# One tile for each PSUM bank of the fill work, and new durations for the scheduler, in an attention kernel with a gated long convolution

The kernel computes an attention layer and a gated convolution behind it. While attention runs, everything else ("fill work") passes through two PSUM banks. The change gives each of these banks a tile of its own, where before two banks were the halves of one tile, and it puts new durations into the small scheduler that orders the instructions.

## Chip, cores, metric

One core of a Trainium2 chip. The metric is the device time of one execution in microseconds (us), lower is better. An execution over 1.5% longer than the kernel's fastest counts as slow. PSUM is the memory that PE writes its products to, used here as eight banks of 512 f32 columns; to evict a bank is to copy it out to SBUF, where the operands lie. Engines: PE multiplies matrices (PEld is its weight load), ACT and DVE work on elements and evict PSUM, POOL works, in this kernel, on elements in SBUF only, SP issues loads and stores.

## The reference

```python
# B,H,S,D = 4,8,768,64; 16 centroids per head
q_assign, k_assign = argmax of normalised q, k against the head's centroids
mask   = q_assign[:, :, :, None] == k_assign[:, :, None, :]
scores = where(mask, q @ k.T / sqrt(D), -1e9)
attn   = softmax(scores) @ v
x      = attn, heads side by side                        # (4, 768, 512)
x1, x2, x3 = split(x @ w_proj)                           # three of 512
conv   = irfft(rfft(x2) * rfft(filter))                  # along the sequence
out    = (x1 * conv * x3) @ w_out
```

The kernel works on 8 groups of 4 heads, two head pairs in each. A pair has 6 steps of 128 keys; a step takes two score products (one per head), an exp on each, and one output product over both. So there are 96 steps. The convolution is done as products with sine and cosine tables.

## The kernel before

The kernel is recorded as a list of operations with planned durations. A list scheduler (`place`) plays them through and fixes the order of the instructions on each engine and the PSUM banks. Semaphores are put in later, by the recording layer, from what each instruction reads and writes.

```python
T.ps = [pp.tile([128, 2, 512], F32, name=f"ps{i}") for i in range(4)]   # 8 banks as 4 pairs

def banks_for(bank, free, st, o):
    if bank.cls == "score":          # both halves of pair 0 or 1
        two = min(((0, 1), (2, 3)), key=lambda p: max(free[p[0]], free[p[1]]))
        return two if max(free[two[0]], free[two[1]]) < 1e8 else None
    if bank.cls == "o":              # output of a head pair
        return (4, 5) if max(free[4], free[5]) < 1e8 else None
    allowed = [6, 7]                 # fill work
    if st.score == 0 and bank.cls == "head":
        allowed += [0, 1, 2, 3, 4, 5]
    elif st.score == st.scores:
        allowed += [0, 1, 2, 3]
        if st.odone == st.otiles:
            allowed += [4, 5]
    ids = sorted((i for i in allowed if free[i] < 1e8), key=lambda i: (free[i], i))[:bank.n]
    return tuple(ids) if len(ids) == bank.n else None

def ap(h):                           # the bank of a fill operation: half of a pair
    return T.ps[h.ids[0] // 2][:, h.ids[0] % 2]
```

A typical fill operation is the projection of the convolution's input, 24 matmuls per batch in six groups of four. Each group fills a bank, and ACT or DVE evicts it:

```python
op(("PE", .87), U, due, r=[...], w=[h], alloc=h)            # 4 matmuls into ap(h)
op(EV512, lambda e, ...: copy(e, T.uv2[:, e_, m], ap(h)), due + 1, r=[h], w=[...], free=[h])
# ... the scheduler frees bank h.ids 0.06 us after the eviction ends, and knows nothing of pairs
```

The softmax here doesn't subtract the row's maximum and nothing guards it: scores larger than these inputs give would overflow.

## Time and profile before

| | |
|---|---|
| time, median of 3 | 521.73 us (520.88 to 522.03) |
| PE busy | 427.9 of 519.7 us, 82% |
| first score, end of the last output product | 36.18 us, 456.99 us |

The page's busy times and its chain of waits (the work that ended last, followed back):

```profile
PE 427.9 (82%) x2444; PEld 179.7 (35%) x2444; DVE 355.5 (68%) x556; ACT 274.5 (53%) x420; POOL 90.5 (17%) x93
...
PE 59%; DVE 21%; ACT 9%; issue 5%; DMA 2%; POOL 1%; POOLq 0%; DVEq 0%; ACTq 0%; SPq 0%
```

Busy time by stretch: the head to the first score, the body to the last output product, the tail. After the stretch come its length and the busy us (with instruction count) of PE, PEld, DVE, ACT and POOL, then the granted PE clock, the DMA share and GB/s:

```profile
core 0: us, PE busy (x) PEld busy (x) DVE busy (x) ACT busy (x) POOL busy (x), PEclk, DMA share, GB/s
0.00:36.18 36.18, 21.61 (x123) 12.93 (x124) 24.59 (x57) 20.36 (x39) 12.59 (x45) 0.91 0.91 193
36.18:456.99 420.81, 361.69 (x2096) 146.98 (x2093) 304.24 (x457) 237.65 (x352) 61.59 (x38) 0.99 0.25 64
456.99:519.67 62.68, 44.62 (x227) 19.78 (x227) 26.66 (x44) 16.51 (x30) 16.27 (x11) 0.89 0.13 51
```

Read the second row: PE idles 420.81 - 361.69 = 59.1 us of the body. The timeline (start, duration, engine, line, operation; in brackets the idle time before it and what ended that) shows what such a hole is made of, in the projection:

```profile
145.50 1.90 PE L587 MATMUL ps<-wpj,uT 128*128 128x512 bf16 x8
...
147.44 0.58 ACT L203 CAST uv<-ps 128x512 bf16<-128x512 f32 x1 [2.04 <-PE ps L587]
...
148.07 1.02 PE L587 MATMUL ps<-wpj,uT 128*128 128x512 bf16 x4 [0.67 <-ACT uv L203]
...
149.13 0.58 ACT L203 CAST uv<-ps 128x512 bf16<-128x512 f32 x1 [1.11 <-PE ps L587]
149.77 1.02 PE L587 MATMUL ps<-wpj,uT 128*128 128x512 bf16 x4 [0.67 <-ACT uv L203]
...
150.83 0.58 ACT L203 CAST uv<-ps 128x512 bf16<-128x512 f32 x1 [1.11 <-PE ps L587]
151.47 1.02 PE L587 MATMUL ps<-wpj,uT 128*128 128x512 bf16 x4 [0.67 <-ACT uv L203]
```

PE waits 0.67 us for ACT, ACT waits 1.11 us for PE, in turn, with nothing else under way on either, though the scheduler gave the groups two banks. And the first eviction starts at 147.44, after all eight matmuls of two groups, not after its own four.

### The profile page before, as it was taken

How to read it: one execution, taken by the hardware profiler on the slowest of the kernel's cores; microseconds unless marked ns; L12 is line 12 of the kernel's file. 1: busy time of each engine (PE TensorE's matmuls, PEld its weight loads, DVE VectorE, ACT ScalarE, POOL GpSimd, SP SyncE). 2: the span in 40 equal slices, each digit the busy share in tenths (PEclk: the TensorE clock that was granted, in tenths of full speed). 3: DMA queues.
4: the chain of work that ended last, by engine and by line, in shares of the span. 5: the costliest groups of instructions: out<-in, count | busy, mean ns of one | idle time of the engine just before them, and what ended most of it. 6: DMA issues, size and time to landing. Idle time of an engine off the chain costs nothing.

```text
span 519.7 us, 6779 instructions
## 1 busy us (share of the span) xinstructions
PE 427.9 (82%) x2444; PEld 179.7 (35%) x2444; DVE 355.5 (68%) x556; ACT 274.5 (53%) x420; POOL 90.5 (17%) x93
## 2 busy tenths in 40 slices
PE   3777899999979787797978888888978799969944
PEld 2342333333323343333323343333423333324421
DVE  7667786798768585675657886676727877663640
ACT  4654468777645465465744466355844455514112
POOL 4220000000005220111003422020101512110541
PEclk9966999999999999999999999999999999979997
DMA  9989005416312132023610213013310000002003
GB/s 209 215 162 232 2 16 142 106 33 138 93 32 67 40 81 45 31 77 112 165 31 12 66 35 88 3 44 106 111 33 4 13 1 32 11 23 121 2 0 122
DMA packets 67226, 37.06 MB, mean 71 GB/s; under 512 B 56636, under 2 KB 62328, under 8 KB 67192
## 3 DMA queue, kind: packets, MB, share of 16 engines
q1 hardware_dynamic: 65992, 34.50, 25.5%
q0 software_dynamic: 1056, 2.10, 2.3%
q8 instruction: 19, 0.31, 0.3%
q14 instruction: 15, 0.12, 0.1%
q10 hardware_dynamic: 144, 0.03, 0.0%
HBM read 30.66 MB, written 6.48 MB: 71 GB/s over the span
## 4 chain that ended last, share of the span: by engine, by line
PE 59%; DVE 21%; ACT 9%; issue 5%; DMA 2%; POOL 1%; POOLq 0%; DVEq 0%; ACTq 0%; SPq 0%
PE ps L475 19%; PE ps L616 8%; PE ps L460 7%; PE ps L661 5%; PE ps L587 4%; PE ps L369 4%; DVE acc L485 4%; DVE tm L600 3%; PE ps L639 3%; PE ps L498 2%; PE ps L387 2%; ACT uv L203 2%; DVE x L623 2%; ACT qkT L203 1%; DMA qkraw<-in_q_dram 1%
## 5 line engine op out<-in xcount | busy, mean ns | idle before, releaser
L464 ACT ACTIVATE p<-ps 128x768 f32<-128x768 f32 x192 | 149.5, 812 | 63.5 <-PE ps L460 46.6
L475 PE MATMUL ps<-p,vraw 128*64 128x385 f32 x768 | 147.0, 503 | 0.4 <-ACT osb L490 0.2
L485 DVE TENSOR_TENSOR acc<-acc,p 128x768 f32<-128x768 f32 x128 | 125.9, 1024 | 6.9 <-ACT p L464 6.7
L460 PE MATMUL ps<-aug,aug 128*128 128x384 bf16 (+1 forms) x384 | 85.7, 331 | 6.6 <-ACT p L464 5.1
L475 PEld LDWEIGHTS ps<-p,vraw 128*64 128x64 f32 x768 | 47.3, 137 | 66.1 <-issue 63.1
L616 PE MATMUL ps<-xT,wpj 128*128 128x384 bf16 x256 | 48.5, 326 | 14.2 <-DVE x L205 3.4
L604 POOL TENSOR_TENSOR y<-tm 128x512 bf16<-128x512 f32 x24 | 36.3, 1520 | 120.2 <-DVE tm L600 119.6
L369 PE MATMUL ps<-ident,qkraw 128*128 128x128 f32 x192 | 36.0, 312 | 22.7 <-DMA qkraw<-in_q_dram 9.0
L649 POOL TENSOR_TENSOR y<-yy,x 128x768 bf16<-128x768 f32 x16 | 32.6, 2035 | 120.2 <-DVE yy L645 79.7
L460 PEld LDWEIGHTS <-aug 128*128 128x128 bf16 (+1 forms) x384 | 33.4, 98 | 50.8 <-issue 37.5
L205 POOL CAST aug<-qkT 64x768 bf16<-64x768 f32 x10 | 10.9, 1086 | 176.7 <-ACT qkT L203 160.4
L369 PEld LDWEIGHTS ps<-ident,qkraw 128*128 128x128 f32 x192 | 23.9, 156 | 43.3 <-ACT qkT L203 10.1
L616 PEld LDWEIGHTS <-wpj 128*128 128x128 bf16 x256 | 23.9, 97 | 41.3 <-issue 25.3
L485 DVE TENSOR_TENSOR acc<-p,p 128x768 f32<-128x768 f32 x32 | 30.1, 964 | 11.0 <-ACT p L464 5.5
L623 DVE TENSOR_TENSOR x<-ps,x 128x384 f32<-128x384 f32 x32 | 17.5, 554 | 25.1 <-PE ps L616 7.8
L600 DVE TENSOR_TENSOR tm<-ps,hm 128x512 f32<-128x512 f32 x48 | 30.9, 682 | 5.4 <-PE ps L347 2.3
L661 PE MATMUL ps<-wout,y 128*128 128x512 bf16 x96 | 25.9, 413 | 9.1 <-POOL y L649 5.2
L587 PE MATMUL ps<-wpj,uT 128*128 128x512 bf16 x96 | 23.3, 379 | 7.8 <-ACT uv L203 7.0
L203 ACT COPY qkT<-ps 128x384 f32<-128x384 f32 x44 | 20.5, 482 | 16.4 <-PE ps L369 12.5
L203 ACT COPY x<-ps 128x384 f32<-128x384 f32 x24 | 11.5, 479 | 33.0 <-PE ps L616 20.0
L203 ACT COPY ob<-ps 128x512 f32<-128x512 f32 x23 | 12.8, 591 | 22.1 <-PE ps L661 15.5
L203 ACT CAST uv<-ps 128x512 bf16<-128x512 f32 x21 | 12.2, 585 | 23.2 <-PE ps L587 18.8
(114 smaller groups left out, 404.5 us busy)
## 6 DMA issues: line engine op xcount, KB each, us to landing
qkraw<-in_q_dram SPq DMA_DIRECT2D x32, 192.0 KB, 5.1
qkraw<-in_k_dram SPq DMA_DIRECT2D x32, 192.0 KB, 4.4
vraw<-in_v_dram SPq DMA_DIRECT2D x8, 768.0 KB, 5.6
rb<-dr SPq DMA_DIRECT2D x30, 192.0 KB, 3.4
out_dram<-ob SPq DMA_DIRECT2D x11, 512.0 KB, 2.6
y<-in_moe_filter_fft_dram SPq DMA_DIRECT2D x4, 384.0 KB, 7.8
wpj<-in_moe_w_proj_dram POOLq DMA_DIRECT2D x1, 1536.0 KB, 11.7
aug<-ohT SPq DMA_DIRECT2D x64, 24.0 KB, 1.9
```

Of the source, the lines that this page charges most:

```text
L203: T.nc.scalar.copy(out, in_)
L369: T.nc.tensor.transpose(ap(h)[:, ts(t, 128)], T.qkraw[s][:, 3 * ch + t].rearrange("p h d -> p (h d)"), T.ident)
L460: T.nc.tensor.matmul(two(h)[:, ch, :384], ag[1][:K, ts(sk, 128)], ag[0][:K, ts(ch, 384)], start=True, stop=True)
L464: ex = op(("ACT", .82 + (1.28 if first[0] is None else 0)), lambda e, h=h, s=s: T.nc.scalar.activation(T.p[s][:, :S].rearrange("p (a b) -> ...
L475: T.nc.tensor.matmul(o[64 * hp:64 * hp + 64, ch, :385], T.vraw[aset][:, 2 * pr + hp, sk * D:(sk + 1) * D], T.p[slots[hp, sk]][:, 384 * ch: ...
L485: T.nc.vector.tensor_tensor(T.acc[hp], x, T.p[slots[hp, sk]][:, :S], op=Alu.add)
L587: T.nc.tensor.matmul(ap(h), f[:, e_, kt, ts(m, 128)], T.wpj[:, kt, DM:2 * DM], start=(kt == 0), stop=(kt == ND - 1))
L600: op(("DVE", .68), lambda e, i=i, cs=cs, r=r, h=h: T.nc.vector.tensor_tensor(T.tm[r][:, cs], ap(h), T.hm[:, i, 2 * r + cs], op=Alu.mult), ...
L604: op(("POOL", 1.36), lambda e, i=i, r=r: T.nc.gpsimd.tensor_tensor(T.y[:, i, r], T.tm[r][:, 0], T.tm[r][:, 1], op=Alu.add), due + 2, r=[(" ...
L616: T.nc.tensor.matmul(ap(h)[:, :384], T.wpj[:, kt, off + dt * 128:off + dt * 128 + 128], T.xT[xs][:, kt, ts(ch, 384)], start=(kt == 0), sto ...
L649: op(("POOL", 1.8), lambda e, dt=dt, xb=xb: T.nc.gpsimd.tensor_tensor(T.y2[:, dt], T.yy[:].rearrange("p t c -> p (t c)"), T.x3[xb][:].rear ...
L661: T.nc.tensor.matmul(ap(h), T.y2[:, kt, ts(2 * tt + e_, 128)], T.wout[:, kt], start=(kt == 0), stop=(kt == ND - 1))
```

## The change

The intent: guard each bank by itself, so that an eviction of one fill bank runs while PE fills the other; and let the scheduler plan with durations nearer to a trace's. The core of the diff (cuts marked):

```diff
-    T.ps = [pp.tile([128, 2, 512], F32, name=f"ps{i}") for i in range(4)]
+    T.bank, T.pair = {}, {}
+    for i in (6, 7):
+        T.bank[i] = pp.tile([128, 512], F32, name=f"bank{i}")
     def ap(h):
-        return T.ps[h.ids[0] // 2][:, h.ids[0] % 2]
+        return bank(h.ids[0])                       # T.bank[i][:]
+class Psum:   # banks 0-3 and 4-5: single tiles, then pairs while scores and outputs
+    ...       # need them, then single tiles again; each turn closes a pool and opens one
 def banks_for(bank, free, st, o):
-    if st.score == 0 and bank.cls == "head":
-        allowed += [0, 1, 2, 3, 4, 5]
+    if st.score == 0:
+        allowed += [0, 1, 2, 3] if bank.cls == "head" else []
+    ...
+    if st.o == 0:
+        allowed += [4, 5] if bank.cls == "head" else []
+    ...       # a first score, a first output and the first fill after them wait for the whole side
-    def place(self, free0, banks_for, switch=0.1, ...
+    def place(self, free0, banks_for, switch=0.08, ...
-            op(("DVE", 2.1), fn, due, ...           # angles of the tables
+            op(("DVE", 2.8), fn, due, ...
-            op(("PE", .84), sim, ...                # likeness to the centroids
+            op(("PE", 1.0), sim, ...
-            op(("PE", 1.28), pv, ...                # output product
+            op(("PE", 1.37), pv, ...
# ... six smaller ones: den .85->.9, rec .45->.52, bc .7->1.15, y 1.36->1.45, I 1.1->1.15, y2 1.8->1.9
```

More of the change, by code (lines that the diff above doesn't have):

```diff
@@ L81, in op, with place @@
         return o
-    def place(self, free0, banks_for, switch=0.1, wait=0.1, rate=215e3):
+    def place(self, free0, banks_for, switch=0.08, wait=0.1, rate=215e3):
         free = dict(free0)
@@ L87, in place @@
         pend = 0
-        st = SimpleNamespace(pool=0.0, dve=0.0, bw=0.0, last=None, score=0, scores=sum(
-            1 for o in self.ops if o.alloc is not None and o.alloc.cls == "score"), otiles=sum(
-            1 for o in self.ops if o.alloc is not None and o.alloc.cls == "o"), odone=0)
+        st = SimpleNamespace(pool=0.0, dve=0.0, bw=0.0, last=None, score=0, o=0, tail=0)
+        st.scores, st.otiles = (sum(o.alloc is not None and o.alloc.cls == c for o in self.ops) for c in ("score", "o"))
         busy = dict.fromkeys(free, 0.0)
@@ L113, in place @@
                             continue
-                        t = max(t, max(bank_free[i] for i in ids))
+                        t = max(t, ids[1])
                     if o.lock and e == "DVE":
@@ L130, in place @@
             if o.alloc is not None:
-                o.alloc.ids = banks_for(o.alloc, bank_free, st, o)
+                o.alloc.ids = banks_for(o.alloc, bank_free, st, o)[0]
                 for i in o.alloc.ids:
@@ L134, in place @@
                 st.score += o.alloc.cls == "score"
+                st.o += o.alloc.cls == "o"
+                if o.alloc.cls not in ("score", "o"):
+                    st.tail |= (st.score == st.scores and min(o.alloc.ids) < 4) + 2 * (
+                        st.o == st.otiles and any(i in (4, 5) for i in o.alloc.ids))
             d = o.eng[e]
@@ L158, in place @@
                         bank_free[i] = h.end + 0.06
-                    if h.cls == "o":
-                        st.odone += 1
             for x in o.eng:
@@ L173, in banks_for, with whole @@
 def banks_for(bank, free, st, o):
+    def whole(lo, hi):
+        return max(free[lo:hi])
     if bank.cls == "score":
         two = min(((0, 1), (2, 3)), key=lambda p: max(free[p[0]], free[p[1]]))
-        return two if max(free[two[0]], free[two[1]]) < 1e8 else None
+        t = max(free[two[0]], free[two[1]]) if st.score else whole(0, 4)
+        return (two, t) if t < 1e8 else None
     if bank.cls == "o":
-        return (4, 5) if max(free[4], free[5]) < 1e8 else None
-    allowed = [6, 7]
-    if st.score == 0 and bank.cls == "head":
-        allowed += [0, 1, 2, 3, 4, 5]
-    elif st.score == st.scores:
-        allowed += [0, 1, 2, 3]
-        if st.odone == st.otiles:
-            allowed += [4, 5]
-    ids = sorted((i for i in allowed if free[i] < 1e8), key=lambda i: (free[i], i))[:bank.n]
-    return tuple(ids) if len(ids) == bank.n else None
+        t = whole(4, 6)
+        return ((4, 5), t) if t < 1e8 else None
+    allowed, first = [6, 7], []
+    if st.score == 0:
+        allowed += [0, 1, 2, 3] if bank.cls == "head" else []
+    elif st.score == st.scores:
+        if st.tail & 1:
+            allowed += [0, 1, 2, 3]
+        elif whole(0, 4) < 1e8:
+            first += [0, 1, 2, 3]
+    if st.o == 0:
+        allowed += [4, 5] if bank.cls == "head" else []
+    elif st.o == st.otiles:
+        if st.tail & 2:
+            allowed += [4, 5]
+        elif whole(4, 6) < 1e8:
+            first += [4, 5]
+    t = lambda i: whole(*((0, 4) if i < 4 else (4, 6))) if i in first else free[i]
+    ids = sorted((i for i in allowed + first if free[i] < 1e8), key=lambda i: (t(i), i))[:bank.n]
+    return (tuple(ids), max(map(t, ids))) if len(ids) == bank.n else None
 def build(T):
@@ L207, in ap, with bank @@
     def ap(h):
-        return T.ps[h.ids[0] // 2][:, h.ids[0] % 2]
+        return bank(h.ids[0])
+    def bank(i):
+        return T.bank[i][:]
     def two(h):
-        return T.ps[h.ids[0] // 2]
+        return T.pair[h.ids[0] // 2]
     EV384 = {"ACT": .48, "DVE": .55}
@@ L280, in fn @@
                 V.scalar_tensor_tensor(r, n, -1.0, n, op0=Alu.mult, op1=Alu.min)
-            op(("DVE", 2.1), fn, due, r=["kc", "s0t", ("x3", 0, 0), ("x3", 0, 1)], w=w, lock=True)
+            op(("DVE", 2.8), fn, due, r=["kc", "s0t", ("x3", 0, 0), ("x3", 0, 1)], w=w, lock=True)
             def sin(e, m=m):
@@ L388, in sim @@
                                        T.qkT[z][:, ch], start=True, stop=True)
-            op(("PE", .84), sim, due, r=[("qkT", z, ch) for z in range(4)] + ["cbd"], w=[h], alloc=h)
+            op(("PE", 1.0), sim, due, r=[("qkT", z, ch) for z in range(4)] + ["cbd"], w=[h], alloc=h, kind="sim")
             op(EV384, lambda e, ch=ch, h=h: copy(e, T.sim[:, ch], ap(h)[:, :384]), due + .8, r=[h], w=[("sim", ch)],
@@ L478, in pv @@
                                            start=(sk == 0), stop=(sk == NT - 1))
-            op(("PE", 1.28), pv, due, r=[("p", slots[0, sk]), ("p", slots[1, sk]), ("vraw", aset), "eps"] +
+            op(("PE", 1.37), pv, due, r=[("p", slots[0, sk]), ("p", slots[1, sk]), ("vraw", aset), "eps"] +
                ([ob] if sk else []), w=[ob], alloc=None if sk else ob, kind="pv")
@@ L499, in den @@
                                        start=True, stop=True)
-        op(("PE", .85), den, te + .5, r=[("acc", 0), ("acc", 1), "ones"], w=[h], alloc=h)
+        op(("PE", .9), den, te + .5, r=[("acc", 0), ("acc", 1), "ones"], w=[h], alloc=h, kind="den")
         op(EV384, lambda e: copy(e, T.den, ap(h)[:, :384]), te + 1.5, r=[h], w=["den"], free=[h])
@@ L510, in rec @@
                 T.nc.vector.reciprocal(T.dn, T.dn)
-            op(("DVE", .45), rec, te + 6, r=[], w=["dn"])
+            op(("DVE", .52), rec, te + 6, r=[], w=["dn"])
             op(("SP", .6), lambda e: T.nc.sync.dma_start(T.dr[os].rearrange("z (a b) -> (z a) b", b=12), T.dn),
@@ L540, in bc @@
                                                T.ident, start=True, stop=True)
-                op(("PE", .7), bc, te + 3, r=["dn"], w=[rk[ch]], alloc=rk[ch])
+                op(("PE", 1.15), bc, te + 3, r=["dn"], w=[rk[ch]], alloc=rk[ch], kind="bc")
             fr = rk
@@ L603, in hyena @@
             for r in range(2):
-                op(("POOL", 1.36), lambda e, i=i, r=r: T.nc.gpsimd.tensor_tensor(
+                op(("POOL", 1.45), lambda e, i=i, r=r: T.nc.gpsimd.tensor_tensor(
                     T.y[:, i, r], T.tm[r][:, 0], T.tm[r][:, 1], op=Alu.add), due + 2, r=[("tm", r, 0), ("tm", r, 1)],
@@ L627, in hyena @@
             due = step(1.1)
-            bk = lambda hh, k: T.ps[hh.ids[k] // 2][:, hh.ids[k] % 2]
+            bk = lambda hh, k: bank(hh.ids[k])
             def I(e, dt=dt, hh=hh):
@@ L640, in I @@
                                            start=(n == 0), stop=(n == 3))
-            op(("PE", 1.1), I, due, r=[("y", i, r) for i in range(3) for r in range(2)] + [("inv", j) for j in range(6)],
+            op(("PE", 1.15), I, due, r=[("y", i, r) for i in range(3) for r in range(2)] + [("inv", j) for j in range(6)],
                w=[hh], alloc=hh)
@@ L648, in hyena @@
                    free=[hh])
-            op(("POOL", 1.8), lambda e, dt=dt, xb=xb: T.nc.gpsimd.tensor_tensor(
+            op(("POOL", 1.9), lambda e, dt=dt, xb=xb: T.nc.gpsimd.tensor_tensor(
                 T.y2[:, dt], T.yy[:].rearrange("p t c -> p (t c)"), T.x3[xb][:].rearrange("p a b -> p (a b)"),
@@ L752, in build, with __init__, turn, want @@
     return P, order
+class Psum:
+    def __init__(self, tc, T):
+        self.tc, self.T, self.state = tc, T, {}
+        for side in ("left", "right"):
+            self.turn(side, 0)
+    def turn(self, side, to):
+        lo, hi = (0, 4) if side == "left" else (4, 6)
+        if side in self.state:
+            self.state[side][1].__exit__(None, None, None)
+        pool = self.tc.tile_pool(name=f"{side}{to}", bufs=1, space=PSUM, side=side)
+        p = pool.__enter__()
+        self.state[side] = (to, pool)
+        if to == 1:
+            for i in range(lo // 2, hi // 2):
+                self.T.pair[i] = p.tile([128, 2, 512], F32, name=f"pair{i}")
+        else:
+            for i in range(lo, hi):
+                self.T.bank[i] = p.tile([128, 512], F32, name=f"bank{i}{to}")
+    def want(self, bank):
+        for i in bank.ids:
+            if i < 6:
+                side = "left" if i < 4 else "right"
+                to = self.state[side][0]
+                if bank.cls in ("score", "o"):
+                    if to == 0:
+                        self.turn(side, 1)
+                elif to == 1:
+                    self.turn(side, 2)
+    def close(self):
+        for _, pool in self.state.values():
+            pool.__exit__(None, None, None)
 @with_exitstack
@@ L815 @@
     ctx.enter_context(tc.manual_schedule())
+    psum = Psum(tc, T)
     for o in order:
+        if o.alloc is not None:
+            psum.want(o.alloc)
         o.fn(o.on)
+    psum.close()
 _INS = ['q', 'k', 'v', 'centroids', 'moe_w_proj', 'moe_filter_fft', 'moe_w_out']
```

## The prediction

> **What bounds the kernel now.** The profile's busy table gives PE 427.9 us of 519.7 (82%), DVE 68%, ACT 53%. The chain that ended last is 59% PE, 21% DVE, 9% ACT, 5% issue. By stretch: between 48 and 462 us (nearly all attention steps) PE is busy 357 of 414 us; in the head (0-48) 28; in the tail (462-520) 43. A step with no fill runs without a hole (scores 0.83 us, then attention-times-value 1.45 us of new time, period 2.21 us). So PE is the bottleneck, and the 57 us in which it idles in the body are what can be won. By length, 50 of these 57 us are gaps of 0.55 us or more, typically 0.65: one eviction (0.48 to 0.585 us) and its semaphores.
>
> **What makes those gaps.** Fill work owns two PSUM banks (6, 7), the two halves of one tile. The waits of the built program, matched with the trace, show that the tile is guarded as a whole: 304 waits (110 on PE, 105 on ACT, 89 on DVE) are on an instruction that touched only the other bank. So matmul into 6, matmul into 7, eviction of 6 and of 7 run in program order, one after the other, though the scheduler plans them as overlapping. The timeline shows it in the projection (four matmuls 1.04 us, hole, four matmuls, hole). Nothing needs this: the Trainium skill, "PSUM — Partial Sum Buffer", section "PSUM bank collisions raise a hardware error", says accesses by two engines to different banks run clean. No run here shows that yet.
>
> **What the change does.** Arithmetic and instruction counts stay (1920 matmuls, the same evictions; PE work 427.9 us by the trace's durations in both orders). In the changed program only a few waits of that kind are left, at the two switches between banks and pairs. The new scheduler durations reorder fill work; PE work before the first score and after the last output product stays 16.6 and 43.2 us. I take their own effect as 0 to 5 us.
>
> **Cost.** Direct loss of these waits (end of the false releaser minus the latest true one): PE 24 us, ACT 49, DVE 39. Following the chain back through these releasers, 130 of its links are of this kind and carry 86 us. That is no saving: with them gone the chain moves to PE's own work. The cap is the body's 57 us; I leave 7 us of short gaps and 15 to 20 us of true waits (score banks not yet freed by exp about 5, denominators 3). Saving: body 30 us, head 3 (of 8 on the chain; loads and the mask's round trip of 5 us stay), tail 1 (1.7 on the chain; it is a serial product-POOL loop).
>
> 521.7 - 34 = 488 us; range 474 to 505. Faster by over 2%: 0.93; within: 0.06; slower: 0.01.
>
> **What would show it.** Body busy share of PE from 86% to about 93%, PE's waits for evictions (ACT uv, x, qkT; DVE x, qkT) nearly gone; projection groups run back to back; busy times unchanged; tail about as long. If the gaps stay, the mechanism is wrong; if they go and time stays, the wait moved to DVE's accumulations or to loads.
>
> **What would make it wrong.** Half-clock stretches at other places (now near 28, 38, 461 and 505 us, each 7 to 10 us long); a new order that starves exp; DVE, near 78% then, becoming the limit.

## More of the kernel before

The groups of instructions that I followed (busy us, mean ns, idle before and its ender):

```profile
L616 PE MATMUL ps<-xT,wpj 128*128 128x384 bf16 x256 | 48.5, 326 | 14.2 <-DVE x L205 3.4
...
L369 PE MATMUL ps<-ident,qkraw 128*128 128x128 f32 x192 | 36.0, 312 | 22.7 <-DMA qkraw<-in_q_dram 9.0
...
L587 PE MATMUL ps<-wpj,uT 128*128 128x512 bf16 x96 | 23.3, 379 | 7.8 <-ACT uv L203 7.0
```

## The result

468.42 us median of 4 (465.83 to 469.18), against 521.88 us for the kernel before in the same rounds: 0.8964, with a 95% interval of 0.8921 to 0.9008. (A ratio is the mean time of one kernel's fast runs over that of the other's of the same rounds, so not quite the ratio of the medians.) The direction was right. The size was not: 53.5 us were saved where 34 were predicted, and the time lies below the stated range (474 to 505).

The page after. Here the chain could be followed through its last 2% only, so I don't read it:

```profile
PE 417.5 (89%) x2431; PEld 180.4 (39%) x2444; DVE 361.4 (77%) x557; ACT 274.3 (59%) x418; POOL 93.0 (20%) x94
...
PE 2%; POOLq 0%; POOL 0%; DVE 0%; ACT 0%; DVEq 0%; issue 0%; ACTq 0%
```

```profile
0.00:34.10 34.10, 18.91 (x123) 11.96 (x124) 28.98 (x64) 21.20 (x38) 13.76 (x46) 0.95 1.02 209
34.10:406.54 372.44, 354.35 (x2086) 148.63 (x2098) 309.33 (x454) 235.57 (x349) 63.83 (x38) 0.98 0.28 72
406.54:467.41 60.87, 44.20 (x224) 19.78 (x227) 23.05 (x41) 17.49 (x31) 15.41 (x11) 0.86 0.13 52
```

The stretches are cut at the same events as before, with the same columns. Head 36.2 to 34.1 us, body 420.8 to 372.4, tail 62.7 to 60.9. So 48.4 us of the 52.3 between the two profiles come from the body. There PE's idle time went from 59.1 to 18.1 us (41.0 less). Its busy time also fell, from 361.7 to 354.4 (7.3 less), for the same 1920 matmul instructions of the program. (The trace shows each f32 matmul of the output products as two records. It has 2431 matmul records against 2444, so a little of that fall may be missing records; a pair of runs with equal counts follows below.) The projection in the changed kernel:

```profile
139.21 0.58 ACT L218 CAST uv<-bank 128x512 bf16<-128x512 f32 x1 [0.96 <-PE bank L605]
...
139.34 1.89 PE L605 MATMUL bank<-wpj,uT 128*128 128x512 bf16 x8
...
140.41 0.69 DVE L220 CAST uv<-bank 128x512 bf16<-128x512 f32 x1
...
141.07 0.49 PE L478 MATMUL pair<-aug,aug 128*128 128x384 bf16 x2
...
141.27 0.58 ACT L218 CAST uv<-bank 128x512 bf16<-128x512 f32 x1 [0.76 <-PE bank L605]
141.39 1.89 PE L605 MATMUL bank<-wpj,uT 128*128 128x512 bf16 x8
...
142.46 0.69 DVE L220 CAST uv<-bank 128x512 bf16<-128x512 f32 x1
```

Eight matmuls of two groups run through in 1.89 us, the scores follow at 141.07, and the next eight at 141.39. The evictions on ACT and DVE (139.21 to 139.79, 140.41 to 141.10) run under the matmuls of 139.34 to 141.23. This is what the Trainium skill asks for in "Perfetto Trace Analysis", section "Matmuls": independent groups should rotate through different PSUM banks, so that the eviction of one overlaps the next group's matmuls. The kernel before did rotate, and did not overlap. The results are correct, so the two banks can be used at once, as the PSUM page quoted in the prediction says.

```profile
L634 PE MATMUL bank<-xT,wpj 128*128 128x384 bf16 x256 | 48.7, 327 | 2.8 <-DVE x L641 1.3
L387 PE MATMUL bank<-ident,qkraw 128*128 128x128 f32 x192 | 34.3, 305 | 11.9 <-DMA qkraw<-in_q_dram 10.7
...
L605 PE MATMUL bank<-wpj,uT 128*128 128x512 bf16 x92 | 22.4, 380 | 0.7 <-DVE uv L220 0.5
```

The idle time before the projection of the gates (L616 before, L634 after), the q and k transposes (L369, L387) and the projection above (L587, L605) fell from 14.2, 22.7 and 7.8 us to 2.8, 11.9 and 0.7. In the transposes 10.7 us of what is left are waits for a load. The largest waits of PE that a term below rests on, two of the body and one of the tail (us in total, times, longest):

```profile
PE bank L387 <- DMA qkraw<-in_q_dram: 5.1, 1, 5.1
PE pair L478 <- ACT p L482: 4.8, 5, 2.3
...
PE bank L516 <- DVE acc L503: 2.7, 1, 2.7
```

### The profile page after: what moved, and what is told of

Read it like the earlier page. It is cut to its first block, busy times and chain, and to the rows that moved or that the text cites. A ratio compares the mean times of both kernels' runs of the same rounds, so it can differ in the third digit from the quotient of the medians.

```text
span 467.4 us, 6821 instructions
## 1 busy us (share of the span) xinstructions
PE 417.5 (89%) x2431; PEld 180.4 (39%) x2444; DVE 361.4 (77%) x557; ACT 274.3 (59%) x418; POOL 93.0 (20%) x94
## 5 line engine op out<-in xcount | busy, mean ns | idle before, releaser
L482 ACT ACTIVATE p<-pair 128x768 f32<-128x768 f32 x192 | 149.2, 811 | 58.8 <-PE pair L478 39.9
L493 PE MATMUL pair<-p,vraw 128*64 128x385 f32 x768 | 147.6, 507 | 1.0 <-DVE hm L350 0.4
L478 PE MATMUL pair<-aug,aug 128*128 128x384 bf16 (+1 forms) x384 | 86.3, 331 | 9.8 <-ACT p L482 4.8
L493 PEld LDWEIGHTS pair<-p,vraw 128*64 128x64 f32 x768 | 48.1, 139 | 66.6 <-issue 61.8
L634 PE MATMUL bank<-xT,wpj 128*128 128x384 bf16 x256 | 48.7, 327 | 2.8 <-DVE x L641 1.3
L387 PE MATMUL bank<-ident,qkraw 128*128 128x128 f32 x192 | 34.3, 305 | 11.9 <-DMA qkraw<-in_q_dram 10.7
L387 PEld LDWEIGHTS bank<-ident,qkraw 128*128 128x128 f32 x192 | 24.1, 154 | 29.5 <-issue 11.9
L618 DVE TENSOR_TENSOR tm<-bank,hm 128x512 f32<-128x512 f32 x48 | 30.5, 680 | 6.0 <-PE bank L365 4.7
L634 PEld LDWEIGHTS <-wpj 128*128 128x128 bf16 x256 | 23.6, 97 | 27.7 <-issue 13.8
L679 PE MATMUL bank<-wout,y 128*128 128x512 bf16 x91 | 26.8, 436 | 7.2 <-POOL y L667 6.0
L218 ACT CAST aug<-qkT 64x768 bf16<-64x768 f32 x28 | 23.2, 830 | 0.7
L605 PE MATMUL bank<-wpj,uT 128*128 128x512 bf16 x92 | 22.4, 380 | 0.7 <-DVE uv L220 0.5
```

Source lines behind the costliest of these rows:

```text
L218: T.nc.scalar.copy(out, in_)
L387: T.nc.tensor.transpose(ap(h)[:, ts(t, 128)], T.qkraw[s][:, 3 * ch + t].rearrange("p h d -> p (h d)"), T.ident)
L478: T.nc.tensor.matmul(two(h)[:, ch, :384], ag[1][:K, ts(sk, 128)], ag[0][:K, ts(ch, 384)], start=True, stop=True)
L482: ex = op(("ACT", .82 + (1.28 if first[0] is None else 0)), lambda e, h=h, s=s: T.nc.scalar.activation(T.p[s][:, :S].rearrange("p (a b) -> ...
L493: T.nc.tensor.matmul(o[64 * hp:64 * hp + 64, ch, :385], T.vraw[aset][:, 2 * pr + hp, sk * D:(sk + 1) * D], T.p[slots[hp, sk]][:, 384 * ch: ...
L605: T.nc.tensor.matmul(ap(h), f[:, e_, kt, ts(m, 128)], T.wpj[:, kt, DM:2 * DM], start=(kt == 0), stop=(kt == ND - 1))
```

## The experiments

Two theories to begin with. A: the guard on pairs, above all on banks 6 and 7, is nearly the whole gain. B: the guard is worth the 34 us I had costed, and the rest comes from the new durations and bank rules, which I had put at 0 to 5 us. The runs went in three calls: the first four after the change; pair67, no_squat and tail_dve; the last four. Across calls they are compared through their ratios to the kernel before.

| run | what it is | median us | ratio to before (95%) |
|---|---|---|---|
| the change | | 468.42 | 0.8964 (0.8921 to 0.9008) |
| split67 | only banks 6 and 7 split | 464.35 | 0.8902 (0.8880 to 0.8924) |
| plan_only | new plan, old pair tiles | 530.38 | 1.0175 (1.0153 to 1.0198) |
| old_durations | the change, durations put back | 461.92 | 0.8865 (0.8844 to 0.8886) |
| one_bank | one fill bank in the body | 578.50 | 1.1096 (1.1038 to 1.1154) |
| pair67 | old_durations, 6 and 7 one tile again | 518.04 | 0.9939 (0.9920 to 0.9958) |
| no_squat | the change, 4 and 5 closed earlier | 464.19 | 0.8895 (0.8875 to 0.8916) |
| full_again | the change, once more | 467.76 | 0.8959 (0.8939 to 0.8979) |
| old_again | old_durations, once more | 462.13 | 0.8856 (0.8837 to 0.8875) |
| no_squat_pv | no_squat, one duration put back | 471.99 | 0.9041 (0.9020 to 0.9062) |
| tail_dve | no_squat, last products on DVE too | 459.76 | 0.8809 (0.8776 to 0.8841) |
| best | old_durations, last products on DVE too | 458.28 (one of five slow) | 0.8769 (0.8749 to 0.8789) |

All gave correct results.

### split67: half of the tiles, nothing else

```diff
-    T.ps = [... for i in range(4)]
+    T.ps = [... for i in range(3)]
+    T.b67 = [pp.tile([128, 512], F32, name=f"bank{i}") for i in (6, 7)]
-        return T.ps[h.ids[0] // 2][:, h.ids[0] % 2]
+        return T.b67[i - 6][:] if i > 5 else T.ps[i // 2][:, i % 2]     # i = h.ids[0]
```

> The kernel before with its own plan and durations; only banks 6 and 7, which fill work uses during attention, are tiles of their own, banks 0 to 5 stay pairs. Theory A (guarding a pair of banks as one tile is nearly the whole of it): 470 to 480 us, PE idle between the first score and the last output product from 59 us to under 25. Rival B (the part of the gain beyond the 34 us predicted comes from the new durations and bank rules): 483 to 492 us.

464.35 us, 6 us below A's range and much further from B's. PE idles 363.10 - 353.12 = 10.0 us in the body:

```profile
34.96:398.06 363.10, 353.12 (x2084) 147.00 (x2093) 303.79 (x457) 237.57 (x352) 61.50 (x38) 0.99 0.28 73
```

Here the chain that ended last can be followed. PE's share of it is 70%, against 59% in the kernel before:

```profile
PE 70%; DVE 16%; ACT 6%; issue 4%; POOL 2%; DMA 1%; POOLq 0%; DVEq 0%; SPq 0%; ACTq 0%
```

Splitting two banks alone beats the whole change. So the rest of the change is no help as it stands, and costs 3 to 4 us.

### plan_only: the new plan with the old tiles

```diff
-        return T.bank[i][:]
+        return T.ps[i // 2][:, i % 2]
-    psum = Psum(tc, T) ... psum.want(o.alloc) ... psum.close()
```

> The changed kernel's plan (new durations, new bank rules, so its instruction order), but the four pair tiles of the kernel before. Theory A: no faster than 515 us, since the waits on the other bank are all back. Rival B: 500 to 512 us, as the better plan helps by itself.

530.38 us: B is out. The new order is 1.75% slower than the old one under the old guard.

### old_durations: the change without its durations

```diff
-    def place(self, free0, banks_for, switch=0.08, ...
+    def place(self, free0, banks_for, switch=0.1, ...
# ... and the nine durations of the diff above
```

> The changed kernel with every scheduler duration put back. Theory A: within 1.5% of the changed kernel (463 to 475 us). Rival B: 480 to 490 us.

461.92 us, a little below A's range: the new durations do not help, they cost 6 us. Compared (full_again and old_again): 467.76 against 462.13. By the ratios old_durations is also 1.9 us ahead of split67, with intervals that just overlap.

### one_bank: is a guarded pair the same as one bank?

```diff
+    body = 0 < st.score < st.scores
-    allowed, first = [6, 7], []
+    allowed, first = ([6] if body and bank.n == 1 else [6, 7]), []
```

> The changed kernel, but from the first score to the last, fill work of one bank may use bank 6 only (the inverse transform, which needs two, still takes 6 and 7). Theory A says that a guarded pair works as one bank, so the time falls back to that of the kernel before: 510 to 528 us. If two guarded banks had still been worth something, this is slower than 528; if the planner's knowing of it counts, it is faster than 510.

578.50 us, outside A's range: my picture of the pair as one bank was too simple. In the body, with the columns of the stretches above:

```profile
34.41:519.10 484.69, 405.28 (x2084) 158.06 (x2098) 303.55 (x455) 236.20 (x354) 47.82 (x31) 0.87 0.21 55
```

PE idles 79.4 us against 59.1 before, in 94 gaps of 0.25 us or more against 77. PE's busy time is 405.3 us against 361.7, and the mean granted clock of the body is 0.87 against 0.99: PE ran at half clock for 129 us of this body, and for 10 us of the body before. So 43.6 of the 63.9 us by which this body is longer than the one before are more busy time of PE, with the clock lower, and only 20.3 us are more idle time. The kernel with the same durations and a guarded pair is plan_only, whose body idles 431.89 - 362.36 = 69.5 us:

```profile
36.14:468.03 431.89, 362.36 (x2086) 149.90 (x2097) 310.23 (x455) 235.59 (x349) 62.24 (x38) 0.98 0.24 62
```

By idle time, then, a guarded pair is worth 10 to 20 us more than one bank; that it is worth the whole difference of the two times is not shown. In a guarded pair two groups can still run one after the other before both are evicted (the 1.90 us of eight matmuls in the timeline before). With one bank no two can. Why the clock fell in this kernel and not in the one before, which idles nearly as large a share of the body (14% against 16%), I did not settle.

### pair67: the guard alone, in one and the same order

```diff
# old_durations, with
+    both = pp.tile([128, 2, 512], F32, name="both")
-        T.bank[i] = pp.tile([128, 512], F32, name=f"bank{i}")
+        T.bank[i] = both[:, i - 6]
```

> old_durations, its order and all its tiles, except that banks 6 and 7 are the two halves of one tile again. The order is the same, so what differs is the guard alone. Theory A: 516 to 528 us. Between the first score and the last output product PE idles 50 to 65 us (old_durations: 12) in over 60 gaps, and is busy 6 to 10 us longer for the same matmuls, since the first matmul after a gap takes about 0.15 us longer than one that follows closely. Rival F (the smaller PE busy time came from the new order): busy within 2 us of old_durations' 354.

518.04 us: A holds, with every number in its range. The scheduler does not see tiles, so the order is that of old_durations and only the guard differs. (The two programs, built again, have the same operations in the same order on every engine.) The bodies of pair67 and of old_durations:

```profile
33.83:454.15 420.32, 361.02 (x2084) 146.98 (x2094) 301.60 (x451) 237.11 (x352) 61.56 (x38) 0.99 0.25 64
```

```profile
34.98:398.75 363.77, 354.13 (x2084) 146.97 (x2094) 301.38 (x451) 237.34 (x352) 61.49 (x38) 0.98 0.29 73
```

The body is 56.6 us longer with the guard. PE idles 59.3 us against 9.6, and is busy 361.0 us against 354.1. There are 77 gaps of 0.25 us or more against 6. (Both traces have 2431 matmul records.) The 6.9 us of busy time are the part that I had not thought of: at the full clock the first matmul of 512 columns after a hole shows 377 ns until its end, and one that follows closely adds 216 ns (medians of the projection). For 384 columns it is 323 ns against 163. This agrees with the Trainium skill, "TensorE: Matmul & The Clock Gate", section "Single matmul latency", which gives (398 + N)/2.4 ns for one matmul by itself on the full clock, an estimate of 379 ns for N = 512. A hole thus costs its idle time and the longer first matmul after it, 0.16 us here. An estimate from these numbers, 71 gaps of 0.16 us, is 11 us; the net measured is 6.9, and the rest of the estimate stays unexplained. The clock is not behind the fall: the body spends 10.2 us at half clock with the guard and 12.8 us without, which works against it. The ends of matmuls are modelled in the profile, so the division between idle and busy leans on that. Their sum, 56.6 us, does not.

### no_squat: where the whole change loses what half of it has

In the changed kernel the first output product starts at 54.74 us, in old_durations at 42.03. The built program shows the reason: before that product, filter spectra go to banks 4, 5, 6, 7, 4 and 5. The new rule leaves 4 and 5 open to such work until the first output, which needs both at once, is placed. The work takes them one at a time.

```diff
     if st.o == 0:
-        allowed += [4, 5] if bank.cls == "head" else []
+        allowed += [4, 5] if bank.cls == "head" and st.score == 0 else []
```

> The changed kernel, new durations and all, but banks 4 and 5 are closed to the filter-spectrum work from the first score on, as in the kernel before. Theory D (that work keeps taking banks 4 and 5 one at a time, so the first output product, which needs both at once, is put off from about 42 to 55 us, and this is why the whole change is slower than old_durations): 460 to 464 us, first product near 42 us. Rival E (the new durations make a worse order throughout): 466 to 470 us.

464.19 us: just above D's range and below E's, with the first product at 43.68 us. The output product's first groups, in the changed kernel and in no_squat:

```profile
54.74 3.85 PE L493 MATMUL pair<-p,vraw 128*64 128x385 f32 x12 [0.41 <-DVE hm L350]
```

```profile
43.68 1.77 PE L493 MATMUL pair<-p,vraw 128*64 128x385 f32 x8
...
46.14 1.52 PE L493 MATMUL pair<-p,vraw 128*64 128x385 f32 x8
```

By the ratios (0.8959 for full_again, 0.8895 here and 0.8856 for old_again, of 522 us) the rule costs 3.3 of the 5.4 us by which the whole change is behind old_durations, which has the same rule but an order in which it does no harm. These are differences of whole orders, good to 1 or 2 us by the intervals. But the traces put the loss where theory D has it: the change starts its first output product 11.1 us after no_squat, is still 7.3 us behind at the 96th of their 768 records (80.7 and 73.4 us), and ends the body with 4.0 us of it (406.5 and 402.6 us). About 2 us are left over.

### full_again, old_again and no_squat_pv: the 2 us left over

```diff
# no_squat, with
-            op(("PE", 1.37), pv, ...
+            op(("PE", 1.28), pv, ...
```

> The whole change once more, on the same chip and in the same rounds as the two next, so that 3 to 7 us between them can be told. 466 to 469 us.

> old_durations once more: 461 to 463.5 us, 4 to 7 us under the whole change. If chips made the difference: within 2 us of it.

> no_squat with one more duration put back, that of the 96 output products (1.37 to 1.28), the most frequent of those changed. If a longer planned product makes the order worse throughout: 461 to 462.5 us, like old_durations. If what is left between no_squat (464.2) and old_durations (461.9) is the head's loads (PE waited 5.6 and 3.1 us for the same qkraw load): 463 to 465.5.

467.76 and 462.13 us: the distance between the change and old_durations is real. But no_squat_pv came to 471.99 us, outside both of its ranges. One planned duration moved by 0.09 us, and the kernel was 7.6 us slower (0.9041 against 0.8895, of 522 us). So the 2 us cannot be put down to any one duration by trying them singly: the list scheduler's order jumps by more than that. They stay open. The traces do exclude the head's loads: no_squat and old_durations start the 288th record of their output products at the same 149.0 us, and are 3.5 us apart at the 384th (202.0 and 198.5).

That the durations became truer is not in doubt for the angles: their six instructions take 151 + 594 + 373 + 534 + 562 + 562 = 2776 ns in the trace before, the old plan said 2.1 us and the new one 2.8. It did not give a faster order.

### tail_dve and best: a version under both kernels

After the last output product comes a serial chain of inverse transform, copy, sum and difference, product y2 on POOL, output projection. In these two runs the last batch's four products may go to DVE as well, in no_squat and in old_durations.

```diff
-            op(("POOL", 1.9), lambda e, ...: T.nc.gpsimd.tensor_tensor(
+            op({"POOL": 1.9, "DVE": 1.05} if last else ("POOL", 1.9), lambda e, ...: (
+                T.nc.vector if e == "DVE" else T.nc.gpsimd).tensor_tensor(
```

> no_squat, and the last batch's four products y2 may run on DVE (1.02 us for that shape) in place of POOL (1.8 us). The tail is a chain of inverse transform, copy, sum and difference, product, output projection; four products 0.8 us shorter each, of which I expect three on the chain: 2 to 3 us less than no_squat. If DVE's own work in the tail (x, yy) is in the way: no gain.

> old_durations, with the last batch's four products y2 open to DVE as in tail_dve: its two gains add, 456.5 to 459.5 us. If the order of the tail differs so that DVE is in the way: 461 to 463.

tail_dve: 459.76 us against 464.19, 4.5 us by the ratios, more than the 2 to 3 expected. Its six runs lie in two clusters, 457.1 to 457.9 and 461.7 to 461.9 us, so the size is good to a few us only. The granted clock divides them: its mean is 0.974 to 0.978 in the lower cluster and 0.959 to 0.963 in the upper one, to which the profiled run belongs. The products in no_squat and in tail_dve:

```profile
438.29 1.81 POOL L667 TENSOR_TENSOR y<-yy,x 128x768 bf16<-128x768 f32 x1 [4.37 <-DVE yy L663]
...
450.26 1.80 POOL L667 TENSOR_TENSOR y<-yy,x 128x768 bf16<-128x768 f32 x1 [1.23 <-DVE yy L663]
```

```profile
438.24 0.96 DVE L667 TENSOR_TENSOR y<-yy,x 128x768 bf16<-128x768 f32 x1
...
447.39 0.96 DVE L667 TENSOR_TENSOR y<-yy,x 128x768 bf16<-128x768 f32 x1
```

From the start of the first product to the end of the fourth are 13.8 us before and 10.1 after: all four are on the chain, at 0.84 us each, and some waits around them went too. best: 458.28 us median of five, 0.8769, within its range and 4.5 us by the ratios below old_again. Four of its runs are 456.65 to 458.37 us. One, the profiled one, took 682.33 us: PE's granted clock was 0.555, or for short stretches 0.5, from 19 us to the end. That run says nothing of the change, and the ratio leaves it out.

## Why the prediction was right or wrong

- **The mechanism was right.** "The tile is guarded as a whole" is shown by pair67 and old_durations: same order, one tile or two for banks 6 and 7, 518.0 or 461.9 us. Of the 304 waits on the other bank counted in the kernel before, split67 still has 56, and it is at 464.4 us.
- **PE as the bound was right.** The body's PE share rose from 86% to 95%, and PE's waits for evictions of the fill banks nearly went (the largest left, for DVE scaling the filter spectra, is 1.5 us). Head (2.1 us measured, 3 predicted) and tail (1.8, 1) were about right, though only roughly comparable: the prediction's head ended at 48 us and its tail began at 462. DVE at 77% did not become the limit.
- **The step that failed is the body's term, "body 30 us".** Measured: 48.4 us. Two parts of it were mis-sized. First, "I leave 7 us of short gaps and 15 to 20 us of true waits": 18.1 us of idle were left, and 9.6 us in old_durations. The two true waits named were about right: 4.8 us for banks not yet freed by exp, and 2.7 for the denominators, which fall into the tail as it is cut here. The other 7 to 12 us I had set aside without a line of the profile behind them, and the short gaps came to 3.8 us (gaps under 0.55 us). What was left besides is one wait of 5.1 us for a load of q at 36 us, which lay in the prediction's head, and some 4 us of smaller waits. Second, "busy times unchanged": PE's busy time in the body fell by 7.3 us, because with each hole goes the longer first matmul after it (pair67: 6.9 us with the order kept). I had cut the body at 48 to 462 us, where PE idled 57 us; cut at first score and last output product it idled 59.1, which is 2 us more of the difference.
- **"I take their own effect as 0 to 5 us"** for the new durations had the wrong sign: they cost 5.4 us, about 3.3 of these by way of the new rule for banks 4 and 5. This loss hid part of the miss, by luck: half of the change, split67, would have been further from the prediction still (57 us saved).
- **"No saving: with them gone the chain moves to PE's own work"**, of the 86 us counted on the chain, was right as far as it can be followed: in split67 PE is 70% of the chain. Those 86 us were too much as a saving, and my cap of 57 us too low, since it held PE's busy time fixed: split67 saves 57.7 us of the body and still idles 10.0 us there.

## What to carry to other kernels

Look whether instructions wait on something that touched another bank of the same tile: buffers that a scheduler plans as two must be two tiles to the layer that sets semaphores. When costing holes on PE, count the longer first matmul after each hole (0.16 us here) as well as the hole, and set no waits aside that no line of the profile shows. When a change brings a fix and a retuned plan together, run each alone: here the smallest piece of the fix was faster than the whole.

## What the Trainium skill lacked or had wrong

- "Perfetto Trace Analysis", section "Matmuls": rotating groups through banks is not enough. Two banks that are halves of one tile were guarded together, and that cost 56.6 us of a 420 us body (pair67 against old_durations). The page doesn't say so.
- "TensorE: Matmul & The Clock Gate", section "Back-to-back issue gap", gives about 131 ns as the sustained spacing of matmuls of 512 columns. Here closely following ones added 216 ns each at the full clock, which is what that section's formula gives for isolated ones.
- The same page, "Part 1: The HAM clock gate", knows the granted clock as 4/8, 8/8, 13/16 once three cores of a die run dense matmuls, and says that it has been seen stuck at 1/4. One execution of best, on one core, ran at 0.555 of the full clock, with 0.5 in between, from 19 us to the end and took 682 us in place of 458. No page that I read has this state.
